# A planned attention and expert kernel: new planner constants, a new ready time for steps on one engine, and a different set-up

## The chip, the cores and the metric

The kernel runs on one core of one Trainium2 chip. The metric is the device time of one execution in microseconds (us); the figures below are medians of several runs, and one further execution was profiled. The engines are PE (matrix products), DVE (vector), ACT (scalar, activations), POOL (general) and SP (which only issues DMAs here); PEld is the loading of PE's weights, which overlaps PE.

## The reference

```python
def _attn_ref(q, k, v, n_sink, window):            # 4 batches, 8 heads, 768 positions, 64 wide
    scores = (1.0 / np.sqrt(D)) * np.matmul(q, k.transpose(0, 1, 3, 2))
    keep = is_sink | in_window                      # 4 sinks, 128 positions back
    scores = np.where(keep, scores, -1000000000.0)
    scores = scores - np.max(scores, axis=-1, keepdims=True)
    a = np.exp(scores)
    a = a / (np.sum(a, axis=-1, keepdims=True) + 1e-09)
    return np.matmul(a, v)

def _moe_ref(x, w_in, w_out):                       # 3072 tokens, 512 -> 2048 -> 512
    h = np.maximum(x @ w_in, 0.0)
    return h * h @ w_out
```

The attention's heads are laid side by side (8 x 64 = 512) and are the tokens of the second part.

## The kernel before, in words

**Tiling.** The 3072 tokens are 8 chunks of 384. A chunk needs the attention of its 4 head pairs (a step s is chunk times 4 plus pair), each of 3 query blocks of 128 rows that see 128 or 256 keys and the 4 sinks: 128 or 260 columns. The product with the weights goes through 16 slices of 128 columns of w_in (L1043), a square on ACT and DVE, and w_out (L1098, L1121). Each product is made of three: one of rounded 32-bit values (xh, wh, gh) and two of 16-bit values (xc, wc, gc) for what the rounding left.

**One attention step.** PE makes scores into a bank of PSUM (L675). DVE masks them and takes the row maximum (L658, a custom instruction followed by an accumulator read). ACT makes the exponentials (L664). ACT prepares the sums and DVE their reciprocals (L724). DVE, ACT or POOL scale the rows (L731, L729). Two small copies put the sinks' weights aside (L744, and the rest of the rounding in L742). PE transposes (L789 the sinks, L861 the rest), ACT or DVE copy back (L524), PE multiplies by v (L954, L960). The result is rounded (L970 on ACT, xh) and what is left taken (L975 on DVE, xc).

**Weights.** A row of the packed weights (32 rows: w_in and w_out of 16 slices) is decoded on DVE by three instructions that follow from one another, L403, L410 and L417; ACT makes wh (L438), one of three engines the 16-bit copy, DVE the rest (L443).

**What sets the order.** All steps go into a `Plan`, each with the engines it may run on, a cost, a rank, and the cells that it reads and writes. `Plan.order` makes a list per engine: for each engine it takes the step that could start first by its own clock, among near ones that of the least rank. When a step is done, those that need it are told when they are ready:

```python
done = t + cost + self.TAIL[e]          # TAIL: DVE 0.09, ACT 0.11, POOL 0.04
x["ready"] = max(x["ready"], free[e] if to_pe and e == "PE" else done + (AHEAD if to_pe else self.HOP))
```

HOP is 0.06. The planner's times are a model; the program that comes out is fixed, one queue per engine, with semaphores. Where PE's model would stand for over 0.4 between 12 and 24 us, the planner puts in products of the identity that nobody uses (L1331, here "fills").

**Set-up, by hand, ahead of the plan.** Two DMAs bring the first k (ACT's queue) and two the first q (SP's, with the parameters `pari` between them); POOL makes index tables and `ident`; DVE makes masks from them (L312 to L322, L349 to L354), and between clears five buffers (L339: VS, PSK_wide, PSK and two SK).

**The end.** DVE writes a number `flagi` (L1324) from a count that PE makes (L1316). All engines read it (L1337) and branch on it to a general path that isn't taken here.

Of the kernel before, what the change touches and what calls it, by code (L numbers as in the profile page):

```python
# [19 lines left out]
P = 128  # L20
# [4 lines left out]
TOK = 384  # L25
NQ = TOK // P
# [8 lines left out]
LOW_POOL = 0.57  # L35
KLOW_DVE = 0.043
KLOW_POOL = -0.16
HOLD = 0
SC_DVE = -0.001
CLAIM = (True, False)  # L40
KS_ACT = 0.37
SOON = 4.111
PS_DVE = -0.1
EARLY = 5
SLOW = 8.5
LAG = 0.548
KEEP = 1.72
STAY = 0.021
LANDS = (3.3, 1.65, 0.6)
VS_POOL = 1.0  # L50
GRAB = 0.853
WARM = (12.0, 24.0)
FULL = 0.75
FIRST = 3.0
URGE = 0
LOW_DVE = 0.0
CP_DVE = 1
SC_ACT = 0.257
ROW = 3.22
TURNED = 2  # L60
RATE = 240.0
LATE = 1.0
AHEAD = 0.2
CHECK = 4
SHORT_ACT = 0.347
SHORT_DVE = 0.409
G16_ACT = -0.07
G16_DVE = 0.564
FULL_DVE = 3.555
TWO = (1.596, -1.602, 1.784)  # L70
THREE = (1, 3.951, 0.051, 3.388)
COLUMN = 14

# [15 lines left out]
def f32(ap):  # L89
    return ap.bitcast(F32)  # L90


class Plan:
# [16 lines left out]
    def add(self, at, rank, emit, reads=(), writes=(), take=(), drop=()):  # L110
        n = len(self.steps)
        before = {self.writer[c] for c in (*reads, *writes) if c in self.writer}
        for c in writes:
            before.update(self.readers.get(c, ()))
        for c in reads:
            self.readers.setdefault(c, []).append(n)
        for c in writes:
            self.writer[c], self.readers[c] = n, []
        before.discard(n)
        for key in drop:  # L120
            self.left[key] = self.left.get(key, 0) + 1
        for b in before:
            self.steps[b]["after"].append(n)
        at = at if isinstance(at, list) else [at]
        self.steps.append(
            dict(at=at, rank=rank, emit=emit, take=take, drop=drop, after=[], waits=len(before), ready=0.0)
        )

    def able(self, s):
        ready, picks = s["ready"], []  # L130
        for pool, key in s["take"]:
            free = [(self.since[i], i) for i in self.items[pool] if self.since[i] is not None and i not in picks]
            if not free:
                return None, None
            t, i = min(free)
            ready = max(ready, t)
            picks.append(i)
        return ready, picks

    def order(self):  # L140
        free = dict(PE=FIRST, DVE=5.75, ACT=6.1, POOL=6.5, SP=1.7, Q=0.0)
        port, landed, mode, flow, held = {"DVE": 0.0, "POOL": 0.0}, [], 0, 0.0, -1.0
        open_ = [n for n, s in enumerate(self.steps) if s["waits"] == 0]
        while open_:
            best = {}
            for n in open_:
                s = self.steps[n]
                ready, picks = self.able(s)
                if ready is None:
                    continue  # L150

                def begin(o):
                    t = max(ready, free[o[0]])
                    if "port" in o or o[0] == "POOL":
                        t = max(t, port["DVE" if o[0] == "POOL" else "POOL"])
                    return t

                e, cost, *kind = min(s["at"], key=lambda o: begin(o) + o[1] + (o[3] if len(o) > 3 else 0.0))
                came = max(ready, free[e])
                t = begin((e, cost, *kind))  # L160
                if e == "SP" and len(landed) > 7:
                    t = max(t, landed[-8])
                best.setdefault(e, []).append((t, s["rank"], n, cost, kind, picks, came))
# [15 lines left out]
            s = self.steps[n]  # L179
# [9 lines left out]
            if e == "SP":  # L189
                flow = max(flow, t + 1.3) + kind[1] / RATE  # L190
                done = max(t + kind[0], flow + 0.7)
                landed.append(done)
                done += LATE
            else:
                done = t + cost + self.TAIL[e]
# [8 lines left out]
            for a in s["after"]:  # L204
                x = self.steps[a]
                to_pe = x["at"][0][0] == "PE"
                x["ready"] = max(x["ready"], free[e] if to_pe and e == "PE" else done + (AHEAD if to_pe else self.HOP))
                x["waits"] -= 1
                if not x["waits"]:
                    open_.append(a)  # L210
# [6 lines left out]
def sink_window_attention_moe(  # L217
# [25 lines left out]
    with ExitStack() as fast:  # L243
# [19 lines left out]
        def first_k(s, queue, n0=0, n1=None):  # L263

            c, p = divmod(s, NPAIR)
            b, half = divmod(c, NHALF)
            kb0, kb1 = max(half * NQ - 1, 0), half * NQ + NQ
            kn = sb(("kn", "KS0", "KS1")[s % 3], [P, 2, 4, BS], F32, f"kn_{s}")
            n1 = n1 or kb1 - kb0
            queue.dma_start(  # L270
                out=kn[:, 0, n0:n1].rearrange("p n c -> p (n c)"),
                in_=k[b, 2 * p : 2 * p + 2, :, kb0 + n0 : kb0 + n1].rearrange("h d n c -> (h d) (n c)"),
            )
# [7 lines left out]
        qn_ = sb("qn", [P, TOK], F32, "qn_0")  # L281
        first_k(0, nc.scalar, 0, 1)
        nc.sync.dma_start(out=qn_[:, 0:P], in_=q[0, 0, :, 0:P])
        nc.sync.dma_start(
            out=pari.rearrange("p a b -> p (a b)"), in_=params.bitcast(I32).partition_broadcast(P)
        )
        first_k(0, nc.scalar, 1, NQ)
        nc.sync.dma_start(out=qn_[:, P:TOK], in_=q[0, 0, :, P:TOK])
        blank = sb("f2", [P, P], F32, "blank")
# [47 lines left out]
        PSKW = sb("w23", [P, 2, NQ, P], F32R, "PSK_wide")  # L337
        for t in (VS, PSKW, PSK, *SK):
            nc.vector.memset(f32(t), 0.0)  # L339

# [12 lines left out]
        nc.vector.tensor_tensor(only, nosink[:, 0:NS], out_[:, 0, 0:NS], op=ALU.is_ge)  # L353
        nc.vector.tensor_copy(parf, pari)  # L354

# [199 lines left out]
        def attention(s, rank):  # L555
# [137 lines left out]
            for m, (i, heads) in enumerate(order):  # L693
                c0, n, mask, o = block(i)
                r = rank(1.9 - 0.8 * m / len(order))
                keys = [("s", s, h, i) for h in heads]
# [50 lines left out]
            for heads in groups:  # L747
                hs = slice(heads[0], heads[-1] + 1)
                r = rank(1.05 if plain or heads[0] else 1.45)
                add(  # L750
# [34 lines left out]
            if turned:  # L785
# [4 lines left out]

                r = rank(0.95)
                add(
# [40 lines left out]
            if turned:  # L833
# [6 lines left out]
                for bi, members in enumerate(parts):  # L840
# [24 lines left out]
                    hs = sorted({h for h, *_ in blocks})  # L865
                    r = rank(0.9 - 0.1 * bi)
                    add(
# [147 lines left out]

        outs = [0]

# [137 lines left out]
        def evacuate(c, f0, f1, t, okey, n):  # L1155
# [12 lines left out]
            if f0 > 0:  # L1168
# [3 lines left out]
                )  # L1172
            for x, cols in enumerate(halves):
                if f0 > 0:
                    add(
# [48 lines left out]

        rows_(range(4), lambda n: n // 2 - 6)
        for s in range(NPAIR):
            attention(s, lambda x, s=s: -60 + 5 * (LAG * s - x))
        row_rank = lambda n: n // 2 - ROW + (0 if n < FH * 2 else FH)
        rows_(range(4, 20), row_rank)
        for s in range(NPAIR, NPS):  # L1230
            attention(s, lambda x, s=s: TWO[0] * (s - NPAIR) + TWO[1] - TWO[2] * x)
        rows_(range(20, NROW), row_rank)
# [82 lines left out]
        def count():  # L1315
# [9 lines left out]
                flagi, bank("flag")[0:1, 0:1], -1.0, float(P), op0=ALU.mult, op1=ALU.add  # L1325
            ), reads=["flag"],
            writes=["flagi"], drop=["flag"],
# [226 lines left out]
```

## Time and profile before

| | |
|---|---|
| median of 3 runs | 646.73 us (646.38 to 646.87) |
| the profiled execution's own time | 646.69 us |
| its span | 644.6 us, so 2.1 us lie around it |
| busy share of the span | PE 99%, DVE 72%, ACT 71%, POOL 25% |
| granted TensorE clock | 0.998 of full, mean |

Times in a trace count from the span's start. A row of the timeline has the start, the time from the first start to the last end of like instructions in sequence, the engine, the line, the operation and what goes in and out. An instruction's start can lie before the end of the one ahead of it on its engine.

### The profile page before, as it was taken

Reading aid. Unit: us, or ns where it says so; the run is one execution under the profiler, and the core shown is the slowest. Engines: PE = TensorE matmul, PEld = TensorE weight load, DVE = VectorE, ACT = ScalarE, POOL = GpSimd, SP = SyncE. Lnnn points to the kernel's source line nnn. Section 1 sums busy time; section 2 is a strip of 40 time slices with the busy share of each in tenths; the row PEclk is TensorE's granted clock in tenths of the full one; section 3 lists DMA queues with packets and bytes.
Section 4 is the critical chain, followed back from the end, with each engine's and each line's share of the span. In section 5 each row is a group of like instructions: output and inputs, shape, how many; then the busy total and the mean of one; then the engine's idle time right before and its main releaser. Section 6 shows DMA issues by size and latency. Waiting matters only on the chain.

```text
span 644.6 us, 12246 instructions
## 1 busy us (share of the span) xinstructions
PE 635.0 (99%) x3748; PEld 422.5 (66%) x3748; DVE 467.2 (72%) x1322; ACT 455.4 (71%) x1413; POOL 159.4 (25%) x330
## 2 busy tenths in 40 slices
PE   8999999999999999999999999999999999999995
PEld 7666656666666766666666666666666666666663
DVE  9999999997667676766777766676678887542232
ACT  6999978877676565656667777777778776656652
POOL 2221122552223333321332222322132222000000
PEclk9999999999999999999999999999999999999999
DMA  8745666547757564664678766666867756222101
GB/s 297 240 148 180 183 224 195 159 116 190 185 131 219 141 189 114 165 183 113 178 218 256 199 195 185 187 201 157 209 174 206 218 143 191 82 98 67 66 17 53
DMA packets 86324, 107.58 MB, mean 167 GB/s; under 512 B 12824, under 2 KB 60440, under 8 KB 86252
## 3 DMA queue, kind: packets, MB, share of 16 engines
q1 hardware_dynamic: 85644, 106.10, 57.3%
q8 instruction: 30, 0.49, 0.3%
q10 hardware_dynamic: 576, 0.60, 0.3%
q14 instruction: 42, 0.34, 0.2%
q0 software_dynamic: 32, 0.05, 0.0%
HBM read 81.34 MB, written 24.38 MB: 164 GB/s over the span
## 4 chain that ended last, share of the span: by engine, by line
PE 94%; DVE 2%; ACT 1%; DMA 1%; issue 0%; SPq 0%; DVEq 0%
PE bank L1043 40%; PE bank L1098 23%; PE bank L1121 17%; PE bank L954 6%; PE bank L681 5%; PE bank L960 1%; PE bank L675 1%; ACT P L664 1%; PE bank L861 1%; DVE P L658 1%; DMA qn<-in_q_dram 1%; DVE wc L443 0%; DVE f L417 0%; PE bank L789 0%; DVE P L731 0%; DVE xc L975 0%
## 5 line engine op out<-in xcount | busy, mean ns | idle before, releaser
L1043 PE MATMUL bank<-xc,wc 128*128 128x384 f16 x1024 | 195.3, 327 | 0.0
L1043 PE MATMUL bank<-xh,wh 128*128 128x384 f32 x512 | 142.1, 377 | 0.0
L1043 PEld LDWEIGHTS <-wc 128*128 128x128 f16 x1024 | 92.9, 98 | 72.3 <-issue 9.9
L664 ACT ACTIVATE P<-P,nbs 128x260 f32<-128x260 f32 (+1 forms) x192 | 93.5, 487 | 46.5 <-DVE nbs L658 41.9
L1057 ACT ACTIVATE r<-bank 128x384 f32<-128x384 f32 x128 | 62.0, 485 | 84.8 <-PE bank L1043 78.7
L731 POOL TENSOR_SCALAR P<-P,small 128x260 f32<-128x260 f32 (+1 forms) x151 | 74.0, 506 | 150.7 <-DVE small L724 134.8
L1098 PE MATMUL bank<-wc,gc 128*128 128x512 f16 x450 | 110.2, 381 | 0.0
L1147 DVE SCALAR_TENSOR_TENSOR bank<-bank,r 128x384 f32<-128x384 f32 x96 | 53.8, 560 | 63.8 <-ACT r L1057 63.5
L1043 PEld LDWEIGHTS bank<-xh,wh 128*128 128x128 f32 x512 | 89.2, 189 | 10.6 <-ACT xh L970 0.3
L1121 PE MATMUL bank<-wc,gc 128*128 128x512 f16 (+1 forms) x350 | 90.2, 363 | 0.0
L1079 DVE TENSOR_TENSOR gc<-bank,gh 128x384 f16<-128x384 f32 x128 | 70.6, 552 | 11.2 <-ACT gh L1062 6.3
L658 DVE CUSTOM_DVE_ANT_0 P<-bank,maskA 128x260 f32<-128x260 f32 x128 | 52.1, 420 | 32.2 <-PE bank L681 31.8
L1121 PE MATMUL bank<-wh,gh 128*128 128x512 f32 (+1 forms) x175 | 70.3, 443 | 0.0
L1098 PEld LDWEIGHTS <-gc 128*128 128x128 f16 x450 | 38.0, 98 | 49.0 <-issue 5.5
L1062 ACT ACTIVATE gh<-r 128x384 fp32r<-128x384 f32 x128 | 66.2, 517 | 3.2 <-PE bank L1121 0.4
L527 POOL CAST gc<-gh 128x384 f16<-128x384 f32 x52 | 26.6, 512 | 158.1 <-ACT gh L1062 146.9
L1098 PE MATMUL bank<-wh,gh 128*128 128x512 f32 x225 | 64.6, 395 | 0.0
L681 PE MATMUL bank<-KS,QS 128*128 128x260 f32 (+1 forms) x288 | 61.8, 305 | 0.0
L681 PEld LDWEIGHTS bank<-KS,QS 128*128 128x128 f32 x288 | 50.2, 189 | 7.8
L890 DVE STREAM_TRANSPOSE T<-P 128x384 f32<-128x384 f32 x96 | 46.4, 496 | 2.8 <-DMA via<-T 1.3
L1121 PEld LDWEIGHTS <-gc 128*128 128x128 f16 x350 | 24.2, 98 | 34.3 <-issue 20.6
L1098 PEld LDWEIGHTS bank<-wh,gh 128*128 128x128 f32 x225 | 40.4, 188 | 3.2
(133 smaller groups left out, 896.9 us busy)
## 6 DMA issues: line engine op xcount, KB each, us to landing
raw<-in_moe_w_dram SPq DMA_DIRECT2D x32, 512.0 KB, 4.2
half<-in_moe_w_dram SPq DMA_DIRECT2D x64, 256.0 KB, 3.3
via<-T SPq DMA_DIRECT2D x96, 96.0 KB, 2.0
PT<-via SPq DMA_DIRECT2D x24, 384.0 KB, 4.0
via<-T SPq DMA_DIRECT2D x96, 80.0 KB, 2.6
PT<-via SPq DMA_DIRECT2D x24, 320.0 KB, 3.9
kn<-in_k_dram SPq DMA_DIRECT2D x28, 264.0 KB, 4.3
qn<-in_q_dram SPq DMA_DIRECT2D x31, 192.0 KB, 3.4
```

The costliest lines, as they stand in the source:

```text
L658: nc.vector.tensor_tensor_reduce(Pt(h)[:, i, o : o + n], ps_[:, 0:n], mask[:, 0:n], -SCALE, BIG, ALU.add, ALU.min, nb)
L664: nc.scalar.activation(Pt(h)[:, i, o : o + n], Pt(h)[:, i, o : o + n], AF.Exp, bias=nb, scale=-1.0, accum_out=sm[:, h, i : i + 1],)
L681: nc.tensor.matmul(bank(key)[:, 0:n], QS(h)[:, cols], flat[:, a, c0 : c0 + n], start=(a == 0), stop=(a == 1),)
L731: {"POOL": nc.gpsimd, "DVE": nc.vector}[engine].tensor_scalar(a, a, rs[:, h, i : i + 1], 1.0, op0=ALU.mult, op1=ALU.mult)
L890: nc.vector.transpose(dst.rearrange("p c j b -> p j c b"), src.rearrange("p j (c b) -> p j c b", b=32))
L1043: nc.tensor.matmul(bank(key)[:, 0:TOK], wt[:, cols], xt, start=(m == 0 and j == 0), stop=(m == len(runs) - 1 and j == len(run) - 1),)
L1057: lambda key=key, r=r: nc.scalar.activation(r(), bank(key)[:, 0:TOK], AF.Relu, scale=R_SCALE),
L1062: lambda gh=gh, r=r, fc=fc: nc.scalar.activation(gh(), r(), AF.Square, accum_out=gsum[:, c % 2, fc : fc + 1]),
L1079: lambda key=key, gh=gh, gc=gc: nc.vector.tensor_tensor(gc()[:, 1], bank(key)[:, 0:TOK], f32(gh()), op=ALU.subtract),
L1098: nc.tensor.matmul(bank(okey)[:, 0:DM], gt, wt, start=(f == f0 and x == 0), stop=False,)
L1121: nc.tensor.matmul(bank(okey)[:, cols], gt, wt[:, cols], start=(f == f0 and j == 0), stop=(f == f1 - 1 and j == 2),)
L1147: nc.vector.scalar_tensor_tensor(full, full, R_SCALE, r, op0=ALU.mult, op1=ALU.mult)
```

## The change

It has four parts. The planner's constants are replaced, some by tuples with a value per step. The planner holds a ready time per engine, and a step whose input comes from its own engine (not SP) is ready when that engine is free, without TAIL and HOP. In the set-up the first k and the first q come in one DMA each, `pari` ahead of q; the five clearings leave DVE: VS and PSK_wide become ACT copies of the blank tile, PSK and the two SK POOL memsets, and a small cast goes from DVE to POOL. The number `flagi` also waits for the last copies out of PSUM (`ends`).

```diff
-KLOW_DVE = 0.043
-KLOW_POOL = -0.16
-HOLD = 0
+KLOW_DVE = 0.545
+KLOW_POOL = 0.639
+HOLD = 0.08
...
-KS_ACT = 0.37
-SOON = 4.111
+KS_ACT = -0.197
+SOON = 4.306
...
-LAG = 0.548
+ONE = (0.241, 1.073, 2.138, 2.161)
...
+STAGES = (2.079, 0.852, 1.028, 1.172, 1.3, 0.085)
+SETUP = (4.3, 5.1, 5.2)
+URGE = 1.167
...
-        free = dict(PE=FIRST, DVE=5.75, ACT=6.1, POOL=6.5, SP=1.7, Q=0.0)
+        free = dict(PE=FIRST, DVE=SETUP[0], ACT=SETUP[1], POOL=SETUP[2], SP=1.25, Q=0.0)
...
-                    t = max(ready, free[o[0]])
+                    t = max(ready, s["ready"][o[0]], free[o[0]])
...
-                to_pe = x["at"][0][0] == "PE"
-                x["ready"] = max(x["ready"], free[e] if to_pe and e == "PE" else done + (AHEAD if to_pe else self.HOP))
+                for to in x["ready"]:
+                    own = to == e and e not in ("SP", "Q")
+                    x["ready"][to] = max(x["ready"][to], free[e] if own else done + (AHEAD if to == "PE" else self.HOP))
...
-        first_k(0, nc.scalar, 0, 1)
-        nc.sync.dma_start(out=qn_[:, 0:P], in_=q[0, 0, :, 0:P])
+        first_k(0, nc.scalar)
...
-        first_k(0, nc.scalar, 1, NQ)
-        nc.sync.dma_start(out=qn_[:, P:TOK], in_=q[0, 0, :, P:TOK])
+        nc.sync.dma_start(out=qn_, in_=q[0, 0, :, 0:TOK])
...
-        for t in (VS, PSKW, PSK, *SK):
-            nc.vector.memset(f32(t), 0.0)
+        nc.scalar.copy(VS, blank.unsqueeze(1).broadcast_to([P, NPAIR, P]))
+        nc.scalar.copy(PSKW.rearrange("p t q c -> p (t q) c"), blank.unsqueeze(1).broadcast_to([P, 2 * NQ, P]))
+        for t in (PSK, *SK):
+            nc.gpsimd.memset(f32(t), 0.0)
...
-        nc.vector.tensor_copy(parf, pari)
+        nc.gpsimd.tensor_copy(parf, pari)
...
-            ), reads=["flag"],
+            ), reads=["flag", *ends],
```

Over the program the fills go from 14 to 7, DVE's instructions from 1403 to 1389, ACT's from 1028 to 1115, POOL's from 390 to 314 (37 16-bit copies of 128x384 go from POOL to ACT, 30 copies for split keys and 9 squares from DVE to ACT).

Lines of the changed program stand 2 to 8 higher than those of the kernel before: L409, L416, L423 are L403, L410, L417; L750, L748 are L744, L742; L664, L730, L737 are L658, L724, L731; L867, L795, L960, L966 are L861, L789, L954, L960; L681 is L675, L1339 is L1331. In brackets stands whose results an instruction waits for; DVE_49 is DVE's own.

DVE in the set-up, before: the clearings stand between the index tables and the masks.

```order
L339 MEMSET VS 128x512
L339 MEMSET PSK_wide 128x768
L339 MEMSET PSK 128x96
L339 MEMSET SK_135 128x384
L339 MEMSET SK_136 128x384
L349 TENSOR_TENSOR outside<-rel,pari 128x128 [waits DMAHW3_49]
L350 TENSOR_TENSOR nosink<-col,pari 128x128
L351 SCALAR_TENSOR_TENSOR mask_97<-outside,nosink 128x128 [waits DVE_49]
L352 TENSOR_TENSOR outside<-rel,pari 128x128
L353 TENSOR_TENSOR only<-nosink,outside 128x4 [waits DVE_49]
L354 CAST parf<-pari 128x4
L658 ISA P_0_186,nbs<-bank_67,mask_97 128x128 [waits PE_49]
```

DVE in the set-up, now: the masks come at once, and the first maximum (L664) behind them.

```order
L355 TENSOR_TENSOR outside<-rel,pari 128x128 [waits DMAHW1_49]
L356 TENSOR_TENSOR nosink<-col,pari 128x128
L357 SCALAR_TENSOR_TENSOR mask_95<-outside,nosink 128x128 [waits DVE_49]
L358 TENSOR_TENSOR outside<-rel,pari 128x128
L359 TENSOR_TENSOR only<-nosink,outside 128x4 [waits DVE_49]
L664 ISA P_0_182,nbs<-bank_67,mask_95 128x128 [waits PE_49]
```

Six instructions of DVE left this place.

DVE at the first weight rows, some 65 instructions into its queue, before: two weight rows (f_276 and f_291) and the sinks' copies of two heads stand in turn.

```order
L744 CAST PSK_wide<-P_0_186 128x2x2x4 [waits DVE_49]
L403 TENSOR_SCALAR f_276<-raw_178 128x512 [waits DMAHW3_49]
L742 TENSOR_TENSOR PSK_wide<-P_0_186,PSK_wide 128x2x4 [waits DVE_49]
L744 CAST PSK_wide<-P_1_188 128x2x2x4
L410 SCALAR_TENSOR_TENSOR f_276<-raw_178,f_276 128x512 [waits DVE_49]
L742 TENSOR_TENSOR PSK_wide<-P_1_188,PSK_wide 128x2x4 [waits DVE_49]
L403 TENSOR_SCALAR f_291<-raw_180 128x512 [waits DMAHW4_49]
L417 SCALAR_TENSOR_TENSOR f_276<-raw_178,f_276 128x512 [waits DVE_49]
L410 SCALAR_TENSOR_TENSOR f_291<-raw_180,f_291 128x512 [waits DVE_49]
```

The same place on DVE now, at the first weight rows (f_318 and f_332).

```order
L409 TENSOR_SCALAR f_318<-raw_176 128x512 [waits DMAHW1_49]
L416 SCALAR_TENSOR_TENSOR f_318<-raw_176,f_318 128x512 [waits DVE_49]
L423 SCALAR_TENSOR_TENSOR f_318<-raw_176,f_318 128x512 [waits DVE_49]
L409 TENSOR_SCALAR f_332<-raw_180 128x512 [waits DMAHW2_49]
L981 TENSOR_TENSOR xc_160<-bank_73,xh_159 128x384 [waits Activation_49]
L416 SCALAR_TENSOR_TENSOR f_332<-raw_180,f_332 128x512 [waits DVE_49]
L423 SCALAR_TENSOR_TENSOR f_332<-raw_180,f_332 128x512 [waits DVE_49]
```

Instructions that wait for the one directly ahead of them now stand back to back (L416 behind L409, L423 behind L416), where before another instruction stood between nearly all of them. Counted over DVE's whole queue, an instruction that waits for a result of the instruction directly ahead of it is found 69 times before and 216 times now; among the first 450 instructions 11 and 76 times. On ACT it is 161 and 366, of the first 450 53 and 102; on POOL 35 and 39.

PE behind the first scores, before: nine fills, then the first transposes, with more fills among what follows.

```order
L1331 MATMUL bank_69<-ident 128x128 x9
L861 MATMUL bank_69<-ident,P_0_186 128x128 x4
L861 MATMUL bank_70<-ident,P_0_186 128x128
L861 MATMUL bank_70<-ident,P_1_188 128x128
L861 MATMUL bank_71<-ident,P_1_188 128x128 x4
L1331 MATMUL bank_72<-ident 128x128
L789 MATMUL bank_72<-ident,PSK_wide 128x128 x2
L1331 MATMUL bank_73<-ident 128x128 x2
L954 MATMUL bank_73<-PT,vn_159 64x128
```

PE behind the first scores, now: the transposes of both head pairs stand first.

```order
L867 MATMUL bank_69<-ident,P_0_182 128x128 x4
L867 MATMUL bank_70<-ident,P_0_182 128x128
L867 MATMUL bank_70<-ident,P_1_184 128x128
L867 MATMUL bank_71<-ident,P_1_184 128x128 x4
L795 MATMUL bank_72<-ident,PSK_wide 128x128 x2
L867 MATMUL bank_69<-ident,P_215 128x128 x4
L867 MATMUL bank_70<-ident,P_215 128x128 x2
L867 MATMUL bank_72<-ident,P_215 128x128 x4
L795 MATMUL bank_71<-ident,PSK_wide 128x128 x2
```

The seven fills that remain stand together 20 rows on, behind the second value product and ahead of the scores of the fourth head pair.

## Rows read from the trace of the kernel before

**Rows 1.** The page: busy time by engine, and the chain that ended last.

```profile
PE 635.0 (99%) x3748; PEld 422.5 (66%) x3748; DVE 467.2 (72%) x1322; ACT 455.4 (71%) x1413; POOL 159.4 (25%) x330
...
PE 94%; DVE 2%; ACT 1%; DMA 1%; issue 0%; SPq 0%; DVEq 0%
```

**Rows 2.** Waits of PE up to 60 us, longest first.

```profile
PE bank L292 <- DVE warm L294: 1.1, 1, 1.1
PE bank L675 <- DMA qn<-in_q_dram: 0.7, 1, 0.7
PE bank L789 <- DVE PSK_wide L742: 0.7, 3, 0.3
```

**Rows 3.** Busy time of each engine by stretch (PE, PEld, DVE, ACT, POOL).

```profile
10.00:100.00 90.00, 89.13 (x575) 57.44 (x573) 89.42 (x263) 83.92 (x240) 18.53 (x33) 1.00 0.64 208
100.00:200.00 100.00, 100.00 (x572) 63.54 (x571) 82.59 (x228) 74.99 (x219) 39.12 (x72) 1.00 0.61 164
```

**Rows 4.** Timeline of PE, DVE around 92 us.

```profile
91.19 0.54 DVE L1079 TENSOR_TENSOR gc<-bank,gh 128x384 f16<-128x384 f32 x1
...
91.55 0.67 PE L1043 MATMUL bank<-xh,wh 128*128 128x384 f32 x2
```

**Rows 5.** Timeline of DVE, three places: pairs of neighbours on the engine.

```profile
1.57 0.23 DVE L315 TENSOR_SCALAR far<-rel 128x128 f32<-128x128 f32 x1
1.83 0.37 DVE L316 TENSOR_TENSOR rel<-rel,far 128x128 f32<-128x128 f32 x1
...
25.70 0.42 DVE L403 TENSOR_SCALAR f<-raw 128x512 int32<-128x512 int32 x1
26.04 0.42 DVE L658 CUSTOM_DVE_ANT_0 P<-bank,maskA 128x260 f32<-128x260 f32 x1
...
105.03 0.41 DVE L403 TENSOR_SCALAR f<-raw 128x512 int32<-128x512 int32 x1
105.48 0.69 DVE L410 SCALAR_TENSOR_TENSOR f<-raw,f 128x512 int32<-128x512 int32 x1
```

**Rows 6.** Timeline of ACT around 37 us.

```profile
36.13 0.45 ACT L970 CAST xh<-bank 128x384 fp32r<-128x384 f32 x1
36.62 0.51 ACT L524 CAST xc<-xh 128x384 f16<-128x384 f32 x1
...
38.58 0.47 ACT L524 CAST SK<-bank 32x384 fp32r<-32x384 f32 x1
38.95 0.48 ACT L1057 ACTIVATE r<-bank 128x384 f32<-128x384 f32 x1
```

**Rows 7.** Timeline of the first 7 us, all engines.

```profile
1.21 0.42 SPq L284 DMA_DIRECT2D pari<-in_params_dram  x1
1.67 0.43 SPq L288 DMA_DIRECT2D qn<-in_q_dram  x1
2.68 0.48 DVE L339 MEMSET VS<- 128x512 f32 x1
3.50 0.80 PE L675 MATMUL bank<-kn,qn 64*128 64x128 f32 x4
4.81 0.23 DVE L349 TENSOR_TENSOR outside<-rel,pari 128x128 f32<-128x128 f32 x1
5.04 2.32 PE L675 MATMUL bank<-kn,qn 64*128 64x260 f32 x10 [0.74 <-DMA qn<-in_q_dram]
5.95 0.28 DVE L658 CUSTOM_DVE_ANT_0 P<-bank,mask 128x128 f32<-128x128 f32 x1
```

**Rows 8.** Timeline of PE behind the first scores.

```profile
11.33 2.27 PE L1331 MATMUL bank<-ident 128*128 128x128 f32 x18
13.44 1.38 PE L861 MATMUL bank<-ident,P 128*128 128x128 f32 x10
```

**Rows 9.** All instructions on the tile flagi: count, shortest/median/longest ns, starts.

```profile
L1337 POOLq TENSOR_LOAD <-flagi x1: 489/489/489, 637.0 to 637.0; - x1
...
L1337 SPq TENSOR_LOAD <-flagi x1: 775/775/775, 638.2 to 638.2; - x1
```

More of the change, by code (lines that the diff above doesn't have):

```diff
@@ L35 @@
 LOW_POOL = 0.57
-KLOW_DVE = 0.043
-KLOW_POOL = -0.16
-HOLD = 0
-SC_DVE = -0.001
+KLOW_DVE = 0.545
+KLOW_POOL = 0.639
+HOLD = 0.08
+SC_DVE = -0.054
 CLAIM = (True, False)
-KS_ACT = 0.37
-SOON = 4.111
+KS_ACT = -0.197
+SOON = 4.306
 PS_DVE = -0.1
@@ L45 @@
 SLOW = 8.5
-LAG = 0.548
[L47 to L51, printed above, removed]
+ONE = (0.241, 1.073, 2.138, 2.161)
+KEEP = 1.633
+STAY = 0
+LANDS = (3.5, 0.05, 2.0)
+VS_POOL = 0
+GRAB = 0
 WARM = (12.0, 24.0)
@@ L54 @@
 FIRST = 3.0
-URGE = 0
+STAGES = (2.079, 0.852, 1.028, 1.172, 1.3, 0.085)
+SETUP = (4.3, 5.1, 5.2)
+URGE = 1.167
 LOW_DVE = 0.0
-CP_DVE = 1
-SC_ACT = 0.257
-ROW = 3.22
+CP_DVE = 0.587
+SC_ACT = 0
+ROWS = (11.315, 4.807, -1, 7.991, 2.159, 2.349, 1.448, 4.112)
 TURNED = 2
@@ L64 @@
 CHECK = 4
[L65 to L72, printed above, removed]
+SHORT_ACT = 0.123
+SHORT_DVE = 0.488
+G16_ACT = 0.077
+G16_DVE = 0.585
+FULL_DVE = 2.476
+TWO = (-1.936, 0.283, 3.036, 0.858, 2.612)
+THREE = (3.281, 4.16, -0.618, 2)
+COLUMN = 9.651
 X_SCALE = 2.0**12
@@ L125, in add @@
         self.steps.append(
-            dict(at=at, rank=rank, emit=emit, take=take, drop=drop, after=[], waits=len(before), ready=0.0)
+            dict(
+                at=at, rank=rank, emit=emit, take=take, drop=drop, after=[], waits=len(before),
+                ready={o[0]: 0.0 for o in at},
+            )
         )
     def able(self, s):
-        ready, picks = s["ready"], []
+        ready, picks = 0.0, []
         for pool, key in s["take"]:
@@ L158, in order @@
                 e, cost, *kind = min(s["at"], key=lambda o: begin(o) + o[1] + (o[3] if len(o) > 3 else 0.0))
-                came = max(ready, free[e])
+                came = max(ready, s["ready"][e], free[e])
                 t = begin((e, cost, *kind))
@@ L694, in attention @@
                 c0, n, mask, o = block(i)
-                r = rank(1.9 - 0.8 * m / len(order))
+                r = rank(STAGES[0] - STAGES[1] * m / len(order) if plain else 1.9 - 0.8 * m / len(order))
                 keys = [("s", s, h, i) for h in heads]
@@ L748, in attention @@
                 hs = slice(heads[0], heads[-1] + 1)
-                r = rank(1.05 if plain or heads[0] else 1.45)
+                r = rank(STAGES[2] if plain else 1.05 if heads[0] else 1.45)
                 add(
@@ L789, in turn_sinks @@
                         nc.tensor.transpose(bank(key)[:, i * P : (i + 1) * P], f32(psk[:, i]), ident)
-                r = rank(0.95)
+                r = rank(STAGES[3])
                 add(
@@ L865, in attention @@
                     hs = sorted({h for h, *_ in blocks})
-                    r = rank(0.9 - 0.1 * bi)
+                    r = rank(STAGES[4] - STAGES[5] * bi)
                     add(
@@ L1013, in dram @@
             return made[name]
-        outs = [0]
+        outs, ends = [0], []
         def products(c, f0, f1, item, checks):
@@ L1173, in evacuate @@
             for x, cols in enumerate(halves):
+                if c == NCHUNK - 1 and t == NQ - 1:
+                    ends.append("T" if x else cell)
                 if f0 > 0:
@@ L1223, in rows_ @@
                     split_steps(n, rank(n))
-        rows_(range(4), lambda n: n // 2 - 6)
+        rows_(range(4), lambda n: n // 2 - ROWS[0])
         for s in range(NPAIR):
-            attention(s, lambda x, s=s: -60 + 5 * (LAG * s - x))
-        row_rank = lambda n: n // 2 - ROW + (0 if n < FH * 2 else FH)
+            attention(s, lambda x, s=s: -60 + 5 * (ONE[s] - x))
+        row_rank = lambda n: n // 2 - ROWS[n // 4] + (0 if n < FH * 2 else FH)
         rows_(range(4, 20), row_rank)
         for s in range(NPAIR, NPS):
-            attention(s, lambda x, s=s: TWO[0] * (s - NPAIR) + TWO[1] - TWO[2] * x)
+            attention(s, lambda x, s=s: TWO[s - NPAIR] - TWO[4] * x)
         rows_(range(20, NROW), row_rank)
```

## The prediction

> **What bounds the kernel now.** I read the page first. PE is busy 99% of the span and makes 94% of the chain that ended last [rows 1], so the time is PE's work plus what PE loses. I looked up what PE loses in the list of its waits: 1.1 us at the first instruction, 0.7 us for q, 0.7 us in three pieces for the sinks' copies [rows 2]; I found no wait of PE between 23 us and the tail. So there is about 2.5 us of waiting to win, plus the fills, and nothing more, however well the other engines are ordered. There is far more to lose, and the table by stretch says where: from 10 to 100 us DVE works 89.42 of 90 us and ACT 83.92, while PE works 89.13 [rows 3]. Three engines are nearly full at once. From 100 us on DVE has 17 of 100 us free and ACT 25 [rows 3]; there PE alone sets the pace. What is lost ahead of 100 us is never made up, since PE has no gap later.
>
> How close is DVE to PE in that stretch? I summed each engine's queue, each instruction at the mean spacing of its group in the trace, up to every result of DVE that PE waits for. The nearest is the subtraction that ends at 91.73 (91.19 + 0.54); the product that needs it is the second of the two in the row that starts at 91.55, at about 91.9 [rows 4]. The slack is some 0.2 us. On DVE these sums follow the trace within 0.6 us up to 110 us.
>
> **The change, part by part.**
>
> *Steps on their own engine.* The planner now counts an own-engine input as ready at once; the program still has the semaphore there, as the bracketed waits in the order show. What such a wait costs when its producer is directly ahead is in the starts of neighbours. L316 needs L315: that one ends at 1.80 and L316 starts at 1.83, 0.03 after. L410 needs L403: end 105.44, start 105.48, 0.04 after. Where the neighbour needs nothing from it, L658 behind L403, the end is 26.12 and the start 26.04, 0.08 before [rows 5]. So a dependent neighbour costs 0.11 to 0.12 us of DVE. ACT shows the same: 0.04 after the end (36.58, 36.62) for the cast of the tile just written, 0.10 before it (39.05, 38.95) for an independent one, 0.14 us apart [rows 6].
>
> The Trainium skill has a rule against this price: "VectorE: DVE Perf Modes", section "The DRAIN you can't avoid", says that a semaphore after each operation costs nothing extra, as the next one waits for the pipeline to empty anyway. The pairs above do not agree, 0.11 us apart. By the rule, this part's term would be 0 and the result that of the "no price" rival below.
>
> Counted in the two orders up to the nearest result, 8 of before's DVE instructions wait for the one directly ahead, and 54 of the 304 up to the nearest result now: 46 more. At 0.11 us that is 5.1 us. Bounds: 0, if the engine stood there anyway for others, and 46 x 0.12 = 5.5. I take 5.1, since DVE is full in this stretch. Of it, 0.6 us fall into what DVE has free between 10 and 100 us (90 - 89.42) [rows 3]: -0.6.
>
> *Set-up.* The clearings lie from 2.68 to 4.81 on DVE [rows 7]; 2.1 us leave it, and the masks end at about 3.8 where they ended at 5.95. But the first maximum also needs scores. PE started the first ones at 3.50 on part of q, and the rest at 5.04, when the q issued at 1.67 had come, 3.4 us after its issue [rows 7]. Now all of q is one DMA, the second on SP's queue; the second was issued at 1.21 before [rows 7], so it lands at about 1.2 + 3.4 = 4.6. The first four records of scores took 0.80 us, and the first maximum can then start near 5.5 instead of 5.95. DVE thus stands for 1.7 of the 2.1 us, and some 0.4 more at the third maximum, since PE starts its later scores hardly earlier. Net: -0.4 to 0 us for DVE; I take -0.1. The copies put on ACT fall in time in which ACT has nothing to do (its first exponential follows the first maximum), those on POOL ahead of its mask; I cost both at nothing, and up to 0.4 us if POOL's mask holds up the third maximum.
>
> *The constants.* They move work. Up to the nearest result DVE's other work, at the spacings of before and without the set-up, is 2.1 us more (two more row scalings, three copies of 16-bit values, one decoding of L443 more, a longer L638), and PE has by then done 0.9 us more of its queue. That makes DVE later by 0 to 1.2 us beside PE; as the sums are off by up to 0.6 us, I take 0.6. The fills drop from 14 to 7. A run of 18 records, 9 fills, lasted from 11.33 to 13.44, so one fill is 0.23 us and seven are 1.6 us [rows 8]. If PE has to wait for DVE, the fills were spent in time that is now waiting, and they win nothing. The 37 + 30 + 9 pieces that ACT gets lie mostly behind 100 us, where it has 25 us of 100 free [rows 3]; nothing for those.
>
> *The number written last.* POOL reads it at 637.0, SP at 638.2 [rows 9]. POOL would read it some 1.3 us later, SP some 0.1 us. The span ends with SP's branch, so I take 0; bounds -0.5 and +1.3, the latter if POOL's branch came to be last.
>
> **The sum.** Own-engine waits +5.1, free time of DVE -0.6, set-up -0.1, moved work +0.6, slack -0.2, end 0: +4.8 us. On the profiled execution's 646.69, which is within 0.1 us of the median, that is 651.5 us.
>
> **The rivals.**
>
> *No price.* If the waits cost nothing, or fall where DVE stands for others anyway, the same sum is -0.1 + 0.6 - 0.2 = +0.3, with DVE back at its old distance from PE: 647.0, no difference. For it: most of the 46 stand in chains whose parts a planner had spread out before, so the same stretch could hold waits for other engines. Against it: DVE had 0.6 us free in 90.
>
> *ACT instead of DVE.* ACT has 49 more waits of this sort among its first 450 instructions; at 0.14 us that is 6.9 us, and it had 90 - 83.92 = 6.1 us free there [rows 3]. If DVE's waits are half hidden by ACT's, so that DVE's term is 2.5 and ACT's overflow about 0.8, the time is 646.7 + 2.5 - 0.6 + 0.8 - 0.2 + 0.3 = 649.5. It speaks for this that both were full; against it, that ACT's results were less near to PE's needs than DVE's.
>
> *The start pays, faster.* If a dependent neighbour costs less than about 0.02 us and the new order keeps PE supplied, PE saves 7 fills (1.6), the three waits for sinks' copies (0.7) and about 0.4 on q [rows 2, 8]. It pays for going over from scores to the long products, in five places instead of one. No row shows that price alone; I bound one by 0 and 0.3, the longest single wait for the sinks' copies [rows 2], and take 1.1 for the four, near the upper end. That is 646.7 - 1.6 - 0.7 - 0.4 + 1.1 = 645.1. PE's rows for the rest of the work are the same. The point from which it decides is 46 x 0.02 = 0.9 us: with more, DVE's lateness eats what the start saved.
>
> **How the numbers follow.** The own-engine waits at nearly full price: 0.50. ACT and half a price: 0.12. No price: 0.18. The start pays: 0.20. A measurement can tell about 0.2% (1.3 us) from no change; so faster 0.20, same 0.18, slower 0.62. The likeliest gives 651.5. Its own range is 649.5 (waits at 60%) to 653.6 (5.5 for the waits, 1.2 for the moved work, 0 for the set-up, 0.4 for POOL's mask, -0.2 of slack, and no free time to fall into). The whole range reaches down to the faster rival, 645.1, and up to 653.6; POOL last at the end would lie beyond it.
>
> **What the changed profile would show.** Right: DVE busy or standing in 0.03 to 0.04 us gaps through 100 us, with L410 and L417 starting after the end of their predecessors; waits of PE for DVE (L1079, L1153, L975 or the sinks' copies), together 5 us or more between 20 and 100 us; the first maximum near 5.5. ACT the cause: PE's waits name ACT's tiles (r, xh, P). Wrong: PE without waits behind 25 us, in which case only the start moved. The prediction falls if the neighbours' gaps are there but PE doesn't wait, for then DVE was not as near as the sums say; or if the gaps are absent, for then the price was read wrongly from three pairs.

## The result and the profile after

The changed kernel takes 654.54 us (median, 654.15 to 655.24), the kernel before beside it 646.78: a ratio of 1.0122 [1.0105, 1.0140], 7.8 us slower. The direction and the mechanism were forecast; the size was 4.8 us, and the range ended at 653.6.

The page of the changed kernel: busy time by engine, and the chain that ended last.

```profile
PE 638.3 (98%) x3734; PEld 422.4 (65%) x3734; DVE 473.1 (72%) x1308; ACT 514.3 (79%) x1501; POOL 115.6 (18%) x254
...
PE 75%; DVE 17%; issue 2%; DMA 2%; ACT 2%; POOL 1%; SPq 0%; DVEq 0%; ACTq 0%; POOLq 0%
```

DVE now makes 17% of the chain where it made 2% [rows 1]: for more than 100 us the end time is set on DVE. The waits of PE, longest first.

```profile
PE bank L681 <- DMA qn<-in_q_dram: 1.4, 1, 1.4
PE bank L867 <- DVE P L737: 1.3, 3, 0.7
PE bank L867 <- POOL P L737: 1.1, 1, 1.1
PE bank L296 <- DVE warm L298: 1.1, 1, 1.1
PE bank L867 <- DVE nbs L664: 0.5, 1, 0.5
PE bank L1127 <- DVE ob L1159: 0.4, 1, 0.4
```

The list names only a part of the loss. Busy time by stretch shows the rest, against 89.13 of 90 and 100.00 of 100 before [rows 3].

```profile
10.00:100.00 90.00, 85.43 (x526) 52.13 (x523) 87.97 (x260) 83.08 (x231) 9.91 (x20) 0.98 0.59 190
100.00:200.00 100.00, 99.39 (x562) 62.37 (x563) 83.35 (x231) 82.55 (x230) 29.64 (x53) 1.00 0.60 169
```

PE stood 4.6 of the 90 us, and stood again behind 100 us, where before it never did. The nearest place is now the output copy of DVE that ends at 99.95 (99.27 + 0.68); PE needs it and starts at 100.01.

```profile
99.27 0.68 DVE L1159 TENSOR_SCALAR ob<-bank 128x512 f32<-128x512 f32 x1
...
100.01 0.50 PE L1127 MATMUL bank<-wh,gh 128*128 128x512 f32 x1 [0.43 <-DVE ob L1159]
```

The first decodings on DVE, one behind the other.

```profile
17.37 0.42 DVE L409 TENSOR_SCALAR f<-raw 128x512 int32<-128x512 int32 x1
17.82 0.69 DVE L416 SCALAR_TENSOR_TENSOR f<-raw,f 128x512 int32<-128x512 int32 x1
18.55 0.69 DVE L423 SCALAR_TENSOR_TENSOR f<-raw,f 128x512 int32<-128x512 int32 x1
19.16 0.42 DVE L409 TENSOR_SCALAR f<-raw 128x512 int32<-128x512 int32 x1
```

17.37 + 0.42 = 17.79, and L416 starts at 17.82, 0.03 after; L423 starts 0.04 after the end of L416. The next L409 takes nothing from L423 and starts 0.08 before its end. Up to 100 us DVE has 59 starts that lie 0.015 to 0.15 us behind the end of the one ahead; before it had 16.

The start, DVE and PE.

```profile
4.09 0.29 DVE L355 TENSOR_TENSOR outside<-rel,pari 128x128 f32<-128x128 f32 x1 [1.00 <-DMA pari<-in_params_dram]
...
4.95 3.39 PE L681 MATMUL bank<-kn,qn 64*128 64x128 f32 x18 [1.38 <-DMA qn<-in_q_dram]
...
5.75 0.29 DVE L664 CUSTOM_DVE_ANT_0 P<-bank,mask 128x128 f32<-128x128 f32 x1 [0.44 <-PE bank L681]
```

The first maximum moved from 5.95 [rows 7] to 5.75. DVE stands 1.0 us for `pari`, which the clearings used to cover, and 0.44 for the scores.

**PE's lost time along its work.** To place the loss I took PE's queue of each kernel, summed its products without the fills (each at the median end-to-end spacing of its kind of pair in the trace of before), and subtracted that sum from the start of the product in the trace. The table gives this difference in us at several amounts of work, and the whole work. The whole work and the last column together lie 6.9 to 7.6 us below the span in every row.

| kernel | whole work | at 20 | 30 | 60 | 100 | 140 | 180 | 600 |
|---|---|---|---|---|---|---|---|---|
| before | 624.0 | 11.4 | 12.5 | 13.2 | 13.3 | 13.6 | 13.3 | 13.2 |
| changed | 625.6 | 14.1 | 14.9 | 17.2 | 18.8 | 19.8 | 20.5 | 19.9 |
| after_free_rows2 | 625.6 | 13.8 | 14.5 | 15.6 | 15.8 | 16.7 | 17.1 | 16.6 |
| after_free_more | 625.6 | 12.9 | 14.0 | 14.8 | 14.9 | 15.5 | 15.4 | 14.9 |
| before_free_rows2 | 624.0 | 11.4 | 12.5 | 13.3 | 13.8 | 14.1 | 13.8 | 13.7 |
| before_priced | 624.7 | 13.2 | 14.1 | 16.0 | 18.1 | 18.3 | 17.8 | 17.8 |
| start_consts | 625.5 | 12.6 | 13.8 | 14.2 | 15.8 | 15.9 | 18.0 | 17.8 |
| late_consts | 625.2 | 11.1 | 13.4 | 14.0 | 14.1 | 14.7 | 14.3 | 13.9 |

By this sum the changed kernel loses 6.7 us more than the kernel before, and its products come to 1.6 us more. That split is not firm: it hangs on how the products are sorted into kinds. Sorted by line, columns, type and place in PE's array, the same sum gives 629.2 us of work before and 628.5 now, and 8.9 us more lost. PE goes from one line's products to another's 572 times before and 569 times now, and behind 200 us, where no stand of PE is listed, the changed kernel's products take 445.8 us for what the mean spacings of before make 446.2. More work on PE is thus not shown. Kernels with one order (the changed one and its two with waits taken away) compare within 0.4 us from 30 on by either sorting; between kernels of different order a difference in the table is good to 2 or 3 us. The fills, some 3.2 us before and 1.6 now, lie in the lost time here.

### The profile page after: what moved, and what is told of

Same layout as the page of the kernel before. It is cut to its first block, busy times and chain, and to the rows that moved or that the text cites. A ratio compares the mean times of both kernels' runs of the same rounds, so it can differ in the third digit from the quotient of the medians.

```text
span 653.1 us, 12076 instructions
## 1 busy us (share of the span) xinstructions
PE 638.3 (98%) x3734; PEld 422.4 (65%) x3734; DVE 473.1 (72%) x1308; ACT 514.3 (79%) x1501; POOL 115.6 (18%) x254
## 4 chain that ended last, share of the span: by engine, by line
PE 75%; DVE 17%; issue 2%; DMA 2%; ACT 2%; POOL 1%; SPq 0%; DVEq 0%; ACTq 0%; POOLq 0%
PE bank L1049 31%; PE bank L1104 23%; PE bank L1127 9%; PE bank L960 5%; PE bank L687 4%; DVE f L416 2%; DVE wc L449 2%; DVE P L664 2%; DVE f L423 2%; DVE gc L1085 2%; DVE f L409 2%; DVE P L737 1%; DMA qn<-in_q_dram 1%; PE bank L966 1%; PE bank L681 1%
## 5 line engine op out<-in xcount | busy, mean ns | idle before, releaser
L1049 PE MATMUL bank<-xh,wh 128*128 128x384 f32 x512 | 144.1, 381 | 0.0
L737 POOL TENSOR_SCALAR P<-P,small 128x260 f32<-128x260 f32 (+1 forms) x147 | 77.3, 542 | 286.8 <-DVE small L730 286.6
L1153 DVE SCALAR_TENSOR_TENSOR bank<-bank,r 128x384 f32<-128x384 f32 x87 | 49.0, 563 | 64.9 <-ACT r L1063 64.5
L1085 DVE TENSOR_TENSOR gc<-bank,gh 128x384 f16<-128x384 f32 x128 | 71.0, 554 | 17.1 <-ACT bank L1151 6.0
L687 PE MATMUL bank<-KS,QS 128*128 128x260 f32 (+1 forms) x288 | 65.9, 314 | 0.2 <-DVE QS L655 0.2
L664 DVE CUSTOM_DVE_ANT_0 P<-bank,maskA 128x260 f32<-128x260 f32 x128 | 52.0, 418 | 13.7 <-PE bank L687 12.8
L687 PEld LDWEIGHTS bank<-KS,QS 128*128 128x128 f32 x288 | 51.7, 189 | 10.0 <-DVE QS L655 0.5
L530 ACT CAST gc<-gh 128x384 f16<-128x384 f32 x108 | 55.0, 509 | 2.8
L896 DVE STREAM_TRANSPOSE T<-P 128x384 f32<-128x384 f32 x96 | 43.5, 486 | 2.7 <-DMA via<-T 2.6
```

Source lines behind the costliest of these rows:

```text
L530: nc.scalar.copy(dst, src) if engine == "ACT" else nc.vector.tensor_copy(dst, src)
L664: nc.vector.tensor_tensor_reduce(Pt(h)[:, i, o : o + n], ps_[:, 0:n], mask[:, 0:n], -SCALE, BIG, ALU.add, ALU.min, nb)
L687: nc.tensor.matmul(bank(key)[:, 0:n], QS(h)[:, cols], flat[:, a, c0 : c0 + n], start=(a == 0), stop=(a == 1),)
L737: {"POOL": nc.gpsimd, "DVE": nc.vector}[engine].tensor_scalar(a, a, rs[:, h, i : i + 1], 1.0, op0=ALU.mult, op1=ALU.mult)
L1049: nc.tensor.matmul(bank(key)[:, 0:TOK], wt[:, cols], xt, start=(m == 0 and j == 0), stop=(m == len(runs) - 1 and j == len(run) - 1),)
L1085: lambda key=key, gh=gh, gc=gc: nc.vector.tensor_tensor(gc()[:, 1], bank(key)[:, 0:TOK], f32(gh()), op=ALU.subtract),
```

## The experiments

**The parts, alone and taken back.** The first four runs separate rule, set-up and constants.

```diff
 # rule_only: before, with the new rule        # after_old_rule: changed, with the old rule
-x["ready"] = max(..., done + (AHEAD if to_pe else self.HOP))
+own = to == e and e not in ("SP", "Q")
+x["ready"][to] = max(x["ready"][to], free[e] if own else done + ...)
...
 # setup_only: before, with the new set-up     # after_old_setup: changed, with the old set-up
-        for t in (VS, PSKW, PSK, *SK):
-            nc.vector.memset(f32(t), 0.0)
+        nc.scalar.copy(VS, blank.unsqueeze(1).broadcast_to([P, NPAIR, P]))
...
-        first_k(0, nc.scalar, 0, 1)
+        first_k(0, nc.scalar)
```

> The kernel before with the planner's new ready rule alone; constants, set-up and end as before. In its first 304 DVE instructions 51 wait for the one directly ahead (before 8, change 57). If those waits are the cause, at 0.11 us each and with DVE full up to 100 us, this alone gives 646.8 + 4.0 to + 8.0, so 651 to 655, with waits of PE for DVE ahead of 100 us. If the new constants or the set-up are the cause, it stays within 1.3 us of 646.8, or becomes faster.

656.70 us, 1.0159 [1.0145, 1.0173]: the rule alone costs 10.2 us, more than the whole change. That is beyond my own range (651 to 655).

> The changed kernel with the old ready rule (input from the own engine counts 0.10 to 0.17 us more on DVE and ACT); constants, set-up and end as changed. 10 of the first 304 DVE instructions wait for the one directly ahead. Own-engine waits as the cause: the loss goes, 645.5 to 648.5. Constants or set-up as the cause: it stays at 652 to 655.

651.05 us, 1.0070 [1.0056, 1.0083]. Taking the rule back gives 3.5 us, not 7.8. Neither expectation fits: with few waits left, the new constants and set-up cost 4.5 us on the old rule.

> The kernel before with the new set-up alone (first q and k in one DMA each, clearings on ACT and POOL, the cast on POOL); planner, constants and end as before. My reading that DVE stands for what it is spared: 646.3 to 647.3, the first maximum at 5.7 instead of 5.95. Set-up as a cause of the loss, since PE now begins its scores at 4.95 where it began at 3.50: 648 to 650. Set-up as a gain of its own: 644.5 to 645.5.

646.70 us, 1.0002 [0.9993, 1.0012]: no difference. By the table's measure PE's lost time is that of before within 0.1 us at every amount of work.

> The changed kernel with the old set-up; planner rule, constants and end as changed. 56 of the first 304 DVE instructions wait for the one directly ahead. Own-engine waits as the cause: within 1.3 us of the changed kernel, 653.3 to 656. Set-up as the cause: 648 to 651.

653.03 us, 1.0108 [1.0092, 1.0123], 1.5 us faster than the changed kernel and just below my bound. So the set-up is free beside the old plan and costs some 1.5 us beside the new one. Beside rule_only, which differs in the constants and the end, it is 3.7 us faster: the constants suit the new rule.

**The waits themselves.** The order stays, the dependence goes. For weight rows 0 to 19 the first two decodings write to room that is unused until then and don't read one another; the third makes a number from the raw word alone, so the weights are others.

```diff
-    f(), raw()[:, :, 1], 3, 0x3FFFFFFF, ...                  # L409
+    fa(), raw()[:, :, 1], 3, 0x3FFFFFFF, ...
-    f(), raw()[:, :, 1], -0x40000000, f(), ...               # L416
+    fb(), raw()[:, :, 1], -0x40000000, raw()[:, :, 0], ...
-    f(), raw()[:, :, 0], 29, f(), ...                        # L423
+    f(), raw()[:, :, 1], -0x43000001, raw()[:, :, 1], ...    # all three for n < 20 alone
```

> The changed kernel, same order on every engine, but for weight rows 0 to 19 the three decodings L409, L416, L423 don't read one another: the first two write to unused room, the third makes a number out of the raw word alone, so the products are of other weights. Dependent neighbours among the first 304 DVE instructions: 31 instead of 57. Own-engine waits as the cause of the loss: 26 x 0.11 = 2.9 us of DVE go, and if DVE sets PE's pace 1.5 to 3.5 us of time, so 651 to 653. If the order is the cause and the waits cost nothing: 654.5, unchanged.

> The same edit on the kernel before, as a control: 14 dependent neighbours instead of 8 among the first 304 (two writings of the unused room now follow one another). Price of the waits: 646.5 to 647.3. If the edit itself changes the times of the decodings or of what follows: outside 645.5 to 647.8.

With these weights the branch's number came out above zero and the general path ran behind, so the times (8958.61 and 9017.32 us) say nothing of the change. The traces do, up to the branch: DVE writes the number at 644.0 where the changed kernel does at 646.3, 2.3 us earlier; the control at 637.3 where before does at 636.8 [rows 9 has its readers, at 637.0]. I ran both again with the number written as 0.

```diff
-                flagi, bank("flag")[0:1, 0:1], -1.0, float(P), op0=ALU.mult, op1=ALU.add
+                flagi, bank("flag")[0:1, 0:1], 0.0, 0.0, op0=ALU.mult, op1=ALU.add
```

> The changed kernel with the decodings of weight rows 0 to 19 cut loose from one another as before (31 dependent neighbours instead of 57 among the first 304 of DVE), and the branch's number written as 0, so that the general path isn't taken. Price of the waits: 26 x 0.11 = 2.9 us off DVE; the trace of the run that branched had PE 2.3 us earlier at the end, so 652.0 to 652.6. Waits free: 654.5.

650.85 us, 1.0068 [1.0056, 1.0081], 3.7 us faster than the changed kernel for 26 waits, 0.14 us each and more than expected. DVE at the same place of the queue as above, and its copy that PE waited for at 99.95 in the changed kernel (99.27 there):

```profile
17.41 0.42 DVE L410 TENSOR_SCALAR fx<-raw 128x512 int32<-128x512 int32 x1
17.75 0.69 DVE L417 SCALAR_TENSOR_TENSOR fx<-raw 128x512 int32<-128x512 int32 x1
18.35 0.69 DVE L426 SCALAR_TENSOR_TENSOR f<-raw 128x512 int32<-128x512 int32 x1
18.95 0.42 DVE L410 TENSOR_SCALAR fx<-raw 128x512 int32<-128x512 int32 x1
...
96.21 0.68 DVE L1162 TENSOR_SCALAR ob<-bank 128x512 f32<-128x512 f32 x1
```

The durations are the same; the starts lie 0.08 to 0.09 us before the end of the one ahead, and from one row's first decoding to the next row's 1.54 us pass instead of 1.79. The copy starts 3.06 us earlier, 0.12 for each wait, and at 100 us of work PE has lost 3.0 us less. Why the whole time gained 0.6 us more than that was not settled.

> The same edit on the kernel before: 14 instead of 8 dependent neighbours, 6 x 0.11 = 0.7 us more of DVE. Price of the waits: 646.9 to 647.4. Waits free: 646.6.

647.14 us, 1.0006 [0.9997, 1.0015]. The control moves by 0.4 us, which the interval doesn't tell from nothing; the table has it 0.5 us later, all of it between 60 and 100.

```diff
 # after_free_more: after_free_rows2, and in L748
-    vec[e].tensor_tensor(to[:, :, 1], src, f32(to[:, :, 0]), op=ALU.subtract)
+    vec[e].tensor_tensor(to[:, :, 1], src, src, op=ALU.subtract)
```

> As after_free_rows2, and the second of the sinks' two copies, L748, reads the attention weights twice instead of what L750 has just written, so its small correction is zero; 22 dependent neighbours among the first 304. Price of the waits: 9 x 0.11 = 1.0 us more off, 651.0 to 652.0. What stays above 646.6 is not in the waits that were taken away: 14 more of them than before, 1.5 us, and the order's own stalls. Waits free: 654.5.

650.39 us, 1.0060 [1.0048, 1.0072], another 0.5 us, half of what was expected. DVE's copy comes 0.83 us earlier still:

```profile
95.38 0.69 DVE L1162 TENSOR_SCALAR ob<-bank 128x512 f32<-128x512 f32 x1
```

By the starts 13 waits are gone here and not 9: of the first 304 instructions 7 start 0.03 to 0.06 behind the end of the one whose result they need in the kernel before, 57 in the changed one, 31 in after_free_rows2 and 18 now. Four of the 22 in the expectation wait for an older result and start 0.05 to 0.08 before the end of the one ahead. The edit also takes such waits from POOL, which makes some of these copies. And in this run's trace the clock does not fall near 26 us, as it does in the changed kernel and in after_free_rows2:

```profile
26.00:29.50 3.50, 3.09 (x23) 1.66 (x20) 3.13 (x9) 3.50 (x11) 0.69 (x1) 1.00 0.40 146
```

The third figure from the end is the granted clock. A run without that fall (after_more_fills, below) was 0.7 us faster with its waits in place, so the 0.5 us are not shown to be the sinks' waits.

Busy time between 60 and 110 us of the changed kernel, of after_free_rows2 and of after_free_more:

```profile
60.00:110.00 50.00, 48.42 (x279) 28.67 (x276) 48.91 (x108) 43.53 (x105) 3.42 (x5) 1.00 0.63 200
```

```profile
60.00:110.00 50.00, 49.96 (x290) 30.15 (x290) 48.76 (x115) 44.66 (x108) 3.66 (x5) 1.00 0.66 204
```

```profile
60.00:110.00 50.00, 50.00 (x290) 30.28 (x289) 48.51 (x115) 44.87 (x110) 3.87 (x5) 1.00 0.66 202
```

PE stood for 1.58 us in this stretch, then 0.04, then not at all; DVE gets through 115 instructions where it got through 108.

**The clock and the fills.**

```diff
+                more = {("turn", 9): 5, ("turn_sinks", 3): 2}.get((name, self.seen[name]), 0)
+                if more:
+                    yield lambda i=picks[0], n=more: self.fill(i, n)
```

> The changed kernel with 7 more unused products of the identity on PE, 5 ahead of the transposes that wait 1.1 us at 24.75 and 2 ahead of the sinks' transposes at 25.85. In the changed kernel the granted clock is 0.5 from 26 to 29.5 us, behind these waits. If the fall of the clock costs what the records at half the clock suggest, 1.7 us, it shows 1.0 there and 652.5 to 653.5 in all. If DVE holds PE anyway, so that a faster PE only waits longer: 654 to 655 with the clock at 1.0. If the fall has another reason: the clock still falls.

653.85 us, 1.0116 [1.0101, 1.0130], 0.7 us below the changed kernel's median, between the two expectations. Stretches of the changed kernel (the third figure from the end is the granted clock):

```profile
22.00:26.00 4.00, 2.45 (x17) 1.38 (x14) 3.96 (x20) 3.97 (x14) 2.26 (x6) 1.00 0.91 288
26.00:29.50 3.50, 3.50 (x12) 1.66 (x11) 3.40 (x8) 3.27 (x10) 0.61 (x1) 0.51 0.16 45
29.50:33.00 3.50, 3.50 (x29) 2.45 (x29) 3.23 (x13) 3.00 (x9) 0.86 (x1) 1.00 0.55 185
```

The same stretch with seven more fills:

```profile
26.00:29.50 3.50, 3.50 (x27) 2.47 (x28) 3.40 (x8) 3.35 (x10) 0.51 (x1) 1.00 0.20 62
```

PE stood 1.55 of 4 us, and then the clock was at 1.2 GHz (0.51) for 3.5 us, in which 12 records of products begin; in the run with the fills 27 do, and the clock stayed at 2.4 GHz. In the table's measure this run is level with the changed one again at 40 us of work, within 0.1 us: what the faster clock won there was spent waiting by then. Of the 0.7 us most appears between 140 and 180, far from the fall, and its cause is open.

```diff
-            for _ in range(n):
+            for _ in range(0):
                 nc.tensor.matmul(banks[i][:, 0:P], ident, ident, start=True, stop=True)
```

> The kernel before without its 14 unused products, same order otherwise. If they only fill time in which PE waits for DVE and ACT: within 0.5 us of 646.6. If they are work on PE's path: 643.5 (14 x 0.23 = 3.2 us less). If they hold the clock up: a stretch of the granted clock at 0.5 shows up ahead of 40 us, and 647.5 to 650.

646.90 us, 1.0004 [0.9995, 1.0013]. The longest wait of PE:

```profile
PE bank L861 <- POOL P L731: 2.2, 1, 2.2
```

The stretch behind it:

```profile
14.00:18.00 4.00, 4.00 (x22) 2.73 (x22) 3.79 (x14) 3.80 (x13) 0.00 (x0) 0.62 1.05 358
```

Without the fills PE stood 2.2 us at once, the clock fell behind it, and the time stayed: the first and third expectations hold in part each, the fall but not its cost.

**What the order costs without waits.**

```diff
 # before_priced: rule_only, and
+PRICE = dict(PE=0.0, DVE=0.11, ACT=0.14, POOL=0.09)
-    free[e] if own else done + ...
+    free[e] + PRICE[e] if own else done + ...
```

> The kernel before with the new ready rule, but an own-engine input counted as ready at the price measured in the trace, 0.11 us on DVE, 0.14 on ACT, 0.09 on POOL after the producer, instead of 0 (or 0.15, 0.17, 0.10 in the old rule). Dependent neighbours 8 of 304, as before. Waits as the cause: 645.5 to 648. If any new order loses, since the constants were chosen with the old rule: 649 to 652.

652.21 us, 1.0082 [1.0068, 1.0097]: 5.6 us lost with as few such waits as before, slightly past the rival's bound. The rival holds here: a planner with a truer price but constants chosen for another loses 5.6 us without the waits. So the 10.2 us of rule_only are not all the price of waits either.

> Old ready rule and old set-up, the number written last, and of the new constants those of the first stages (ONE, STAGES, SETUP, URGE, HOLD, KEEP, STAY, LANDS, GRAB, VS_POOL, SC_DVE, SC_ACT, CP_DVE and ROWS for the first 20 weight rows). 9 dependent neighbours among the first 304 of DVE, as before. If the remaining loss is made by the order of the first stages: 649.5 to 651, PE late before 60 us. If by the later constants: 646 to 647.5.

652.67 us, 1.0092 [1.0078, 1.0107]: 6.1 us, beyond the expectation.

> Old ready rule and old set-up, the number written last, and of the new constants those of the later stages (TWO, THREE, COLUMN, SOON, SHORT, G16, FULL_DVE, KLOW, KS_ACT and ROWS from row 20 on). 9 dependent neighbours. If the order of the first stages makes the remaining loss: 646 to 648, PE late only behind 60 us. If the later constants make it: 649.5 to 651.

648.25 us, 1.0029 [1.0017, 1.0040]: 1.7 us, just past the expected 648, and PE is late ahead of 60 already (14.0 against 13.2 at 60). On the old rule the new constants of the first stages cost most; start_consts loses part of it ahead of 100 us of work and 2.1 us between 140 and 180.

> The kernel before with the branch's number written last, nothing else. My term for it: 0, so 646.3 to 647.0. If POOL's or PE's later reading moves the end: 647.3 to 648.0.

646.71 us, 0.9999 [0.9990, 1.0009]: nothing, as said.

## Why the prediction was right in kind and short in size

**What bounds it: right.** DVE was 0.2 us from holding PE, and a DVE that is later makes PE late for good: no kernel in the table gets back more than 0.8 us of what it had lost. One reading was off: a piece of PE's waiting for the sinks' copies lies behind the 23 us from which I found none.

```profile
32.77 0.44 PE L789 MATMUL bank<-ident,PSK_wide 128*128 128x128 f32 x2 [0.17 <-DVE PSK_wide L742]
```

**Own-engine waits, 5.1 us: right, and about half of it shown.** By their starts the first 304 DVE instructions hold 50 more of them, 57 against 7. Up to the copy at 99.27 it is 54, and before up to its nearest result 7, where I had 8: 47 more instead of 46. With the order kept, 26 taken away gave 3.7 us, while the control did not move clear of noise. Thirteen more came with 0.5 us and with another clock, so their share is open. The 11 that are left over before's would be 1.3 us at 0.12 each, which is worked out, not run. The Trainium skill ("VectorE: DVE Perf Modes", section "The DRAIN you can't avoid") states from eight copies that a semaphore after each costs nothing extra. These runs don't agree where the next instruction needs the result: 26 such waits made 3.7 us.

**The deductions: wrong.** This is the first of two steps that failed. I had subtracted 0.6 us since DVE had that much free time, and another 0.6 by halving the moved work. Of DVE's 0.58 us free between 10 and 100, 0.22 were six gaps of 0.03 to 0.06, and 0.36 were two stands at 18.96 and 42.45. Neither absorbs waits that sit elsewhere: in the changed kernel DVE stands longer, 2.3 us in stands over 0.15 us ahead of 100 us (0.6 before), of which 1.9 at the start. Undeducted the sum is 6.0 us. At the nearest place PE was 7.2 us late by sums: 100.01 less 83.46 of PE's queue up to there, fills counted, against 91.9 less 82.5 at the place of before. The two places lie in different orders, so this is good to 2 or 3 us. What the moved work cost by itself was not run.

**Nothing lost from 100 us on: wrong.** This is the second step that failed. The range's upper end, 6.9 us, already leaves the free time and the halving out; what it lacks is this loss and most of the set-up's 1.5 us beside the new plan (below). I had set this term at nothing because DVE and ACT had time to spare there. PE loses 1.7 us more between 100 and 180 of its work (18.8 to 20.5), with DVE at 83%. A mean of 83% doesn't show single stands. With the rows cut loose 1.3 us remain of it, with the sinks as well 0.5 (14.9 to 15.4), so the waits seem to make most of that too. With 1.2 us for the deductions and 1.7 us for this, the sum of 4.8 becomes 7.7 against the 7.8 measured; that they meet so closely is luck in part, as the set-up's 1.5 us is not in it and the waits' price was not run for all of them.

**Set-up, -0.1: right alone, for a partly other reason.** 646.70 against 646.52. DVE stood for `pari`, not only for the scores. Beside the new plan it costs 1.5 us. Some 0.4 of it is in the start, at the third maximum, in the changed kernel and in after_old_setup:

```profile
6.73 0.43 DVE L664 CUSTOM_DVE_ANT_0 P<-bank,mask 128x260 f32<-128x260 f32 x1 [0.47 <-PE bank L681]
```

```profile
6.37 0.42 DVE L664 CUSTOM_DVE_ANT_0 P<-bank,mask 128x260 f32<-128x260 f32 x1
```

The old plan has a cast of VS (L542) at this place, which ran from 6.36 in setup_only and needs no scores. The rest of the 1.5 us was not settled.

**The fills: right.** They cover waiting; taking all 14 out of the kernel before changes nothing measurable. That PE pays more for going over I had only in the faster rival, at 1.1 us, and no run shows it.

**The rivals.** No price and the paying start are out by after_free_rows2. ACT as the bound is not seen: its share of the chain is 2%. The number written last is 0.

**What remains.** After 39 waits are gone 3.7 us are left. The 11 waits that are left on DVE (1.3, worked out) make a third of it; the rest is open. The order of the first stages may be part of it, but start_consts was run on another rule and loses more than that, so it doesn't measure it. ACT has 50 more such waits among its first 450 instructions, and no run took those away, so their share is not known. How the 7.8 us divide between rule and constants has no single answer: the rule costs 10.2 with the old constants and 3.5 with the new.

## What to carry to other kernels

An instruction that reads the result of the one directly ahead on its own engine cost about 0.12 us on DVE here; a list scheduler that takes it as free will put such chains back to back (216 against 69 here), and where that engine was within 0.2 us of holding the critical one, 26 such waits were paid in full. Count those neighbours in the order of a new program before trusting a new rule. When a sum of rows is at hand, take free time or "half" off it only with a row that shows where the free time lies, and set no stretch at nothing by its mean alone. Constants chosen for one planner can't be judged on another: new ones on the old rule lost 4.5 us here, old ones on a new rule 5.6.

## What the runs showed of the hardware

The granted clock fell to half after PE had stood 1.55 of 4 us, and in the kernel before without its fills after PE had stood 2.2 us at once. Neither fall came with more than 0.7 us: PE was waiting for other engines around both, and in the changed kernel its lost time is the same soon after with the fall and without. DVE's table casts at the start took 0.75 and 0.62 us where they took 0.28 and 0.15 before (0.76 and 0.63 in setup_only); behind them DVE waited for `pari`, so that cost nothing here. Why they took longer was not settled.
